# Attention and two feed-forward layers on one core: two totals by accumulating DMA, a second layer without plain products, another plan

## The chip, the cores and the metric

One NeuronCore of a Trainium2 chip. The metric is the device time of one execution in microseconds, as the median of the runs shown.

## What is computed

The inputs are q, k, v of 4 x 8 heads, 576 positions, 64 wide, and a gate value f per position. Attention has a causal mask and a decay from the running sum of log f; its output, 2304 tokens x 512, goes through two feed-forward layers, all in float32:

```
attn  = softmax(scale * q @ k.T + cum[i] - cum[j], causal) @ v
x     = attn.transpose(0, 2, 1, 3).reshape(2304, 512)
h     = x @ w_in            # 512 x 2048
x     = (h - tanh(h)) @ w_out
h     = x @ w_in2
out   = (h * sigmoid(h)) @ w_out2
```

## The kernel before, in words

Every float32 number of a product is split into a high part in TensorE's rounded float32 format and a low rest, and each product is made of three matmuls: high x high, high x low, low x high. ScalarE makes the high part (a cast), VectorE the low one (a subtraction).

**Units.** Each layer (l = 0, 1) is cut into 12 units: four sets s of 512 hidden columns by three blocks b of 768 tokens. Units are numbered 0 to 11 for the first layer and 12 to 23 for the second. A unit has a first product (x by w_in), the gate, and a second product (gate output by w_out), which is added to a total of the block in the big SBUF tile `x`. Both products are done in seven half-size products on 2 x 2 blocks in place of eight, in a scheme of Winograd's kind: sums and differences of the blocks are multiplied, and the products combined. The four quarters of a block are called 11, 12, 21, 22.

**The joint part.** Units 0 to 2 run beside and after the attention in written-out steps. From unit 3 on, `joint()` writes a list of tasks: in the stage that starts at `base[u]`, TensorE does by turns one group of unit u's first product (`h_step`, 12 matmuls of 384 columns) and one group of unit u-1's second product (`c_step`, 12 matmuls of 384 columns in the first layer, 18 of 256 in the second). A stage has 14 such steps. Around them stand the tasks of the other engines: ScalarE copies a bank of partial sums to the other bank (`cp`, `seed`), runs the gate function and casts; VectorE combines gate outputs (`two`), makes low halves, adds to totals (`gain`); both decode the next weights (`decode`, spread over the stage by `spread`).

**The plan.** `planned()` is a list scheduler. It knows a cost per task in steps, what each task reads and writes, and a due time (`latest`) that follows from the step at which TensorE needs the result. It takes tasks in order of time, on each engine the one that is due first among those that are ready; TensorE's and the DMAs' tasks keep their written order. If a task would hold up another that becomes ready during it and is due before its end, the other goes first (`soon`). The result is only an order of instructions on each engine; on the chip, semaphores do the waiting. All DMAs of this part are issued by SP, in the plan's order. The plan starts with every engine free at time 0, though units 0 to 2 still have work in flight there.

**Unit 13 (PLAIN).** Its second product is done with the eight plain half-size products: groups of 24 or 12 matmuls of 256 columns (`plain_c`, line 764), with one weight block of its own (`GROUPS[2][2]`, placed at 11), four gate operands in place of seven, no combinations of gate outputs, and its four totals copied by ScalarE (line 1076). Its stage is one step longer (line 826).

**Between the layers.** The last set of the first layer (units 9 to 11, one per block) ends with four VectorE instructions, `mix` (line 1058): the difference of quarters 22 and 21 into the tile `aside`, 22 plus 12 into 22, and the last partial sums into 12 and 21. SP stores `aside` to DRAM. The stage of unit 12, 13 or 14 then begins with `make` (line 892): it loads `aside` into quarter 11, makes `t` = 12 - 11 and 21 = 21 - t on VectorE (line 900), and splits seven operands into a ring of three tiles (cast at line 915, low half at line 912), each of which SP also stores for later sets (`spill`, line 638). `t` is kept in the tile `f_tmp`, which in the first layer is the temporary of the last two tanh gates of each unit (lines 943, 944). The first second-product group of unit 12 writes the bank that the last two mixes of block 2 read; before it, line 720 sets half of that bank to zero.

Of the kernel before, what the change touches and what calls it, by code (L numbers as in the profile page):

```python
# [7 lines left out]
F32 = mybir.dt.float32  # L8
# [6 lines left out]
P = 128  # L15
B, H, S, D = 4, 8, 576, 64
# [14 lines left out]
NB, TB, TH = 3, 768, 384  # L31
NPR = NFC // 2
NSET = NPR // 2
# [3 lines left out]

U0 = 3
S0 = U0 // 3
PLAIN = (13,)  # L40
PLAINSETS = {s for s in range(NSET, 2 * NSET) if all(NB * s + b in PLAIN for b in range(NB))}
EARLIER = 5
MIXED = {u // NB for u in PLAIN} - PLAINSETS
# [5 lines left out]
def forgetting_attention_two_ffn(  # L49
# [12 lines left out]
    nc = tc.nc  # L62
# [103 lines left out]
    PLUS, MINUS = ALU.add, ALU.subtract  # L166
# [270 lines left out]
    def gather(n):  # L437
        u, h, j, i, g = halves[n]
        l, s, b = units[u]
        acc = accs.pop((u, h, g))  # L440
        t0 = TB * b + TH * h
        if l == 0:
            total, acc = x[:, 2 * g:2 * g + 2, t0:t0 + TH], acc[:, :, 0:TH]
        else:
            total = x[:, 2 * h:2 * h + 2, TB * b + 512 * g:TB * b + 512 * g + (512, 256)[g]]
            total = total.rearrange("p k (t w) -> p k t w", w=256)
            acc = acc[:, 0:2 - g].rearrange("p t (k w) -> p k t w", w=256)
        if s == 0:
            nc.scalar.copy(total, acc)
        else:  # L450
            nc.vector.tensor_tensor(total, acc, total, ALU.add)
# [210 lines left out]
    aside = {}  # L662
# [12 lines left out]
    def aside_load(b, to):  # L675
        nc.sync.dma_start(out=to, in_=aside[b])

    gring = {}

    def gtile(n):  # L680
# [125 lines left out]
    def joint():  # L806
# [6 lines left out]
        def task(when, eng, cost, fn, reads=(), writes=(), keen=False):  # L813

            tasks.append((when, eng, cost, fn, reads, writes, keen))
# [76 lines left out]
        def make(u):  # L892

            b, t0 = units[u][2], base[u]
            at = {"21": (1, 0), "22": (1, 1), "11": (0, 0), "12": (0, 1)}
            q = {c: lambda c=c: xblock(b, *at[c]) for c in at} | {"t": lambda: ftile(u, "tmp")}
            key = dict(zip(q, [("x", b, c) for c in (11, 12, 21, 22)] + ["tmp"]))

            def total(when, to, p, r, op=MINUS):
                task(t0 + when, "V", W2, lambda: tt_(q[to](), q[p](), q[r](), op), (key[p], key[r]), (key[to],))  # L900

            task(t0 - 4, "D", 3, lambda: aside_load(b, q["11"]()), (("t1", b),), (key["11"],))
            total(-1.5, "t", "12", "11")
            total(0, "21", "21", "t")
            src = {1: "11", 2: "21", 6: "t", 3: "12", 7: "22", 5: "11", 4: "21"}
            for k, i in enumerate(STEPS):
                n, f = 7 * (u - U0) + k, src[i]
                kr, when = ("xr", n % 3), t0 + 2 * k - 4.6

                def low(n=n, f=f):  # L910
                    t = ring_tile(n)
                    tt_(t[:, 1], q[f](), rd(t[:, 0]), MINUS)
                    spill(n)

                task(when, "A", N2, lambda n=n, f=f: copy(ring_tile(n)[:, 0], q[f]()), (key[f],), (kr,))
                task(when + 0.1, "V", W2, low, (key[f], kr), (kr,))


        for u in range(U0, len(units) + 1):
            t0 = base[u]  # L920
            if u < len(units):
# [27 lines left out]
                def two(when, to, p, r, op, kt, kp, kr, keen=True):  # L949
                    task(when, "V", W2, lambda: tt_(to, p, r, op), (kp, kr), (kt,), keen)  # L950
# [3 lines left out]
                cp(t0 + 5.05, zs, ys, kz, ky)  # L954
                cp(t0 + 7.05, g12, zs, f12, kz)
                cp(t0 + 9.05, g22, ys, f22, ky)
                two(t0 + 11.05, g22, zs, g22, PLUS, f22, kz, f22)
                two(t0 + 11.5, g12, zs, g12, PLUS, f12, kz, f12)
                gate(t0 + 11.55, g22, g22, f22, f22, True)
                gate(t0 + 12.0, g12, g12, f12, f12, True)  # L960
                if u in PLAIN:
# [78 lines left out]

            if l == 0:
                if s == S0:
                    task(t0 + 3, "V", W2, lambda a=xs[12], c=xs[22]: tt_(a, a, c, MINUS), (kx[12], kx[22]), (kx[12],))
                else:
                    task(t0 + 2, "D", 3, lambda b=b: aside_load(b, aside_tile()), (("t1", b),), ("aside",))
                    task(t0 + 10.9, "A", N2, lambda to=ys: copy(to, aside_tile()), ("aside",), (ky,), True)
                seed(t0 + 2.05)
                gain(t0 + 4.05, 11, zs, kz)
                seed(t0 + 6.05)
                gain(t0 + 8.05, 22, zs, kz)  # L1050
                task(t0 + 8.9, "A", N2, lambda to=zs, frm=xs[12]: copy(to, frm), (kx[12],), (kz,), True)
                gain(t0 + 10.05, 21, ys, ky)
                gain(t0 + 12.05, 12, zs, kz, copies=True)
                if s < NSET - 1:
                    task(t0 + 14.05, "A", N2, lambda frm=ys: copy(aside_tile(), frm), (ky,), ("aside",), True)
                else:
                    def mix(when, to, frm, r, op, keys, kt):
                        task(when, "V", W2, lambda: tt_(to() if callable(to) else to, frm, r, op), keys, (kt,))

                    mix(t0 + 11.5, aside_tile, xs[22], xs[21], MINUS, (kx[22], kx[21]), "aside")  # L1060
                    mix(t0 + 12.5, xs[22], xs[22], xs[12], PLUS, (kx[22], kx[12]), kx[22])
                    mix(t0 + 14.05, xs[12], xs[12], ys, MINUS, (kx[12], ky), kx[12])
                    mix(t0 + 14.06, xs[21], xs[21], ys, PLUS, (kx[21], ky), kx[21])
                task(t0 + (14.5 if s < NSET - 1 else 13), "S", 0, lambda b=b: aside_store(b), ("aside",), (("t1", b),))
                continue
            first = s == 0
            if plain_:
# [59 lines left out]
    def planned(tasks):  # L1127

        LAG, EARLY = 0.1, 8

        def lag(n, d):

            e, f, keen = tasks[n][1], tasks[d][1], tasks[n][6]
            if e == f:
                return 0.06 if e == "V" else 0
            return LAG if keen or e == "P" else LATE.get((f, e), LAG)

        LATE = {("V", "A"): 0.5, ("A", "V"): 0.15, ("P", "A"): 0.1, ("P", "V"): 0.1}
        tasks = sorted(tasks, key=lambda t: t[0])
        writer, readers, deps = {}, {}, []  # L1140
        for n, (when, eng, cost, fn, reads, writes, keen) in enumerate(tasks):
            d = {writer[k] for k in reads if k in writer}
            for k in writes:
                d |= readers.pop(k, set())
                if k in writer:
                    d.add(writer[k])
            d.discard(n)
            deps.append(d)
            for k in reads:
                readers.setdefault(k, set()).add(n)  # L1150
            for k in writes:
                writer[k] = n
        free, end, order = dict.fromkeys("PAVSD", 0.0), {}, []
        queue = {e: [n for n, t in enumerate(tasks) if t[1] == e] for e in free}


        latest = [t[0] if t[1] == "P" else 1e9 for t in tasks]
        for n in reversed(range(len(tasks))):
            for d in deps[n]:
                if tasks[d][1] != "P":  # L1160
                    latest[d] = min(latest[d], latest[n] - lag(n, d) - tasks[d][2])

        def ready(n):
            if all(d in end for d in deps[n]):
                return max([end[d] + lag(n, d) for d in deps[n]] + [tasks[n][0] - EARLY])

        behind = 0
        while any(queue.values()):
            best = None
            for e, waiting in queue.items():  # L1170
                known = [(max(r, free[e]), n) for n in waiting[:1 if e in "PSD" else 60] if (r := ready(n)) is not None]
                if not known:
                    continue
                t = min(known)[0]
                now = [n for r, n in known if r <= t]
                n = min(now, key=lambda n: latest[n])

                soon = [(r, k) for r, k in known if t < r < t + tasks[n][2] - 0.1 and latest[k] + behind < t + tasks[n][2]
                        and latest[n] + behind > r + tasks[k][2]]
                if soon:  # L1180
                    t, n = min(soon)
                if best is None or t < best[0]:
                    best = t, e, n
            t, e, n = best
            if e == "P":
                behind = t - tasks[n][0]
            queue[e].remove(n)
            end[n] = t + tasks[n][2]
            free[e] = t if e == "D" else end[n]
            order.append((t, e != "P", len(order), n))  # L1190
        return [tasks[n][3] for *_, n in sorted(order) if tasks[n][3]]
# [438 lines left out]
```

## Time and profile before

| | us |
|---|---|
| median of 3 runs | 904.29 (904.21 to 904.33) |
| the profiled execution | 904.37 |
| its span, first to last instruction | 902.6 |
| busy: PE | 890.4 (99%) |
| busy: PEld | 845.5 (94%) |
| busy: DVE | 784.9 (87%) |
| busy: ACT | 602.4 (67%) |
| busy: POOL | 161.6 (18%) |

PE is TensorE's matmuls, PEld its weight loads, DVE VectorE, ACT ScalarE, POOL GpSimd, SP the engine that issues DMAs. The profiled execution is one more run; its span leaves out what comes before the first and after the last instruction. The granted clock of TensorE is 1.000 over the whole span. Matmuls are pipelined, and the ends in the rows are modelled, so a matmul's row is longer than the step from one to the next.

### The profile page before, as it was taken

To read this page: it belongs to the slowest core of one execution; us is meant where nothing else is said; L and a number is where in the kernel's file an instruction comes from. 1 tells how busy PE (TensorE), PEld (TensorE's weight loads), DVE (VectorE), ACT (ScalarE), POOL (GpSimd) and SP (SyncE) were. 2 spreads that over 40 slices of the span, in tenths; PEclk is the share of its full clock that TensorE was granted. 3 is DMA by queue.
4 is the path that set the end of the run, shared out by engine and by line. 5 is a ranking of instruction groups with operands and counts; after the bars stand their busy time and mean duration, and the time that the engine had idled before them with its cause. 6 is when DMAs were issued, how large, how long until landed. Compare 5 with 4: busy or idle time off the path is not lost.

```text
span 902.6 us, 16281 instructions
## 1 busy us (share of the span) xinstructions
PE 890.4 (99%) x6080; PEld 845.5 (94%) x6080; DVE 784.9 (87%) x1321; ACT 602.4 (67%) x1006; POOL 161.6 (18%) x242
## 2 busy tenths in 40 slices
PE   8999999999999999999999999999999999999997
PEld 6777777799999999999999999999999999999997
DVE  7799999798889999998999999997897799776647
ACT  6888888765556666766676777866765666555443
POOL 8999999400000000000000000000000000000000
PEclk9999999999999999999999999999999999999999
DMA  5424533567458677787678565677667566555753
GB/s 167 155 98 150 177 119 102 191 250 281 193 224 285 244 264 247 246 296 270 228 275 293 208 243 221 249 252 278 242 239 264 196 234 226 191 191 177 233 169 123
DMA packets 51103, 196.04 MB, mean 217 GB/s; under 512 B 9744, under 2 KB 15120, under 8 KB 50992
## 3 DMA queue, kind: packets, MB, share of 16 engines
q1 hardware_dynamic: 50744, 194.72, 60.9%
q8 instruction: 48, 0.79, 0.3%
q10 hardware_dynamic: 280, 0.28, 0.1%
q14 instruction: 31, 0.25, 0.1%
HBM read 151.98 MB, written 41.88 MB: 215 GB/s over the span
## 4 chain that ended last, share of the span: by engine, by line
PE 94%; DVE 3%; ACT 1%; issue 1%; POOL 0%; DMA 0%; DVEq 0%; POOLq 0%; ACTq 0%
PE h L656 33%; PE a L735 32%; PE t L1362 5%; PE s L1315 5%; PE a L431 5%; PE out_t L1418 5%; PE h L475 3%; PE a L764 2%; PE s L1307 2%; PE h L461 1%; PE out L1418 0%; PE out_t L1446 0%; DVE x L1035 0%; ACT raw L203 0%; DVE gr L991 0%
## 5 line engine op out<-in xcount | busy, mean ns | idle before, releaser
L656 PE MATMUL h<-xr,wh 128*128 128x384 f32 x1176 | 299.0, 335 | 1.0 <-ACT h L947 0.9
L656 PEld LDWEIGHTS h<-xr,wh 128*128 128x128 f32 x1176 | 208.6, 188 | 1.6 <-ACT h L947 1.6
L656 PE MATMUL h<-xr,wl 128*128 128x384 f32 x588 | 196.6, 334 | 0.0
L656 PEld LDWEIGHTS h<-xr,wl 128*128 128x128 f32 x588 | 110.4, 188 | 0.0
L990 ACT CAST gr<-f 128x768 fp32r<-128x768 f32 x104 | 86.8, 838 | 32.5 <-PE a L735 29.8
L991 DVE TENSOR_TENSOR gr<-f,gr 128x768 fp32r<-128x768 f32 x104 | 98.7, 951 | 5.8 <-ACT gr L990 5.7
L735 PE MATMUL a<-wh,gr 128*128 128x256 f32 x516 | 99.2, 282 | 0.0
L735 PEld LDWEIGHTS a<-wh,gr 128*128 128x128 f32 x516 | 82.9, 190 | 0.0
L1336 ACT ACTIVATE p<-p,mn 128x128 f32<-128x128 f32 (+3 forms) x128 | 71.2, 558 | 17.0 <-DVE mn L1328 14.3
L1035 DVE TENSOR_TENSOR x<-a,x 128x768 f32<-128x768 f32 (+1 forms) x64 | 59.3, 929 | 20.7 <-PE a L735 20.5
L735 PE MATMUL a<-weh,gr 128*128 128x256 f32 x384 | 74.0, 282 | 0.3 <-DVE x L1035 0.3
L1350 POOL TENSOR_SCALAR p<-p,sm 128x128 f32<-128x128 f32 (+3 forms) x128 | 73.0, 587 | 7.2 <-DVE sm L1347 6.8
L735 PE MATMUL a<-gr,wh 128*128 128x384 f32 x288 | 73.3, 334 | 0.4 <-DVE gr L991 0.4
L735 PE MATMUL a<-wl,gr 128*128 128x256 f32 x258 | 72.8, 282 | 0.0
L1328 DVE CUSTOM_DVE_ANT_0 p<-s,mask 128x128 f32<-128x128 f32 (+3 forms) x128 | 59.6, 479 | 14.2 <-PE s L1315 14.1
L1027 ACT COPY a<-a 128x768 f32<-128x768 f32 x49 | 38.4, 783 | 47.1 <-PE a L735 45.5
L735 PEld LDWEIGHTS a<-weh,gr 128*128 128x128 f32 x384 | 61.7, 190 | 0.6 <-issue 0.5
L947 ACT COPY h<-h 128x768 f32<-128x768 f32 x42 | 33.0, 786 | 34.7 <-PE h L656 33.5
L735 PE MATMUL a<-gr,weh 128*128 128x384 f32 x216 | 54.8, 334 | 0.0
L735 PE MATMUL a<-wel,gr 128*128 128x256 f32 x192 | 54.2, 282 | 0.0
L1257 POOL TENSOR_TENSOR kqs<-kqraw,kqs 128x288 fp32r<-128x288 f32 (+1 forms) x62 | 53.8, 890 | 1.3
L735 PEld LDWEIGHTS a<-gr,wh 128*128 128x128 f32 x288 | 52.0, 188 | 0.7 <-DVE gr L991 0.7
(169 smaller groups left out, 2070.0 us busy)
## 6 DMA issues: line engine op xcount, KB each, us to landing
xr<-xd SPq DMA_DIRECT2D x126, 768.0 KB
raw<-w_in SPq DMA_DIRECT2D x32, 512.0 KB
raw<-w_out SPq DMA_DIRECT2D x32, 512.0 KB
xd<-xo SPq DMA_DIRECT2D x21, 768.0 KB
xd<-xr SPq DMA_DIRECT2D x21, 768.0 KB
kqraw<-kq SPq DMA_DIRECT2D x16, 608.0 KB
aside<-aside SPq DMA_DIRECT2D x15, 384.0 KB
vraw<-v SPq DMA_DIRECT2D x16, 320.0 KB
```

What stands on the lines that cost most here:

```text
L431: nc.tensor.matmul(dst, w, m, start=first and r == 0, stop=last and r == 2)
L656: nc.tensor.matmul(dst[:, j, 0:TH], w[:, ds], m[:, d], start=i in (1, 5) and d == r == 0, stop=d == 1 and r == 2, skip_group_check=True,)
L735: nc.tensor.matmul(dst, w, m, start=fresh and (l == 0 or d != 1) and j == r == 0, stop=j == 1 and r == 2, skip_group_check=True,)
L990: task(w, "A", N2, lambda g=g, f=frm: copy(g[:, 0], f), (kf,), (("gh", kg),))
L991: task(w + 0.1, "V", W2, lambda g=g, f=frm: tt_(g[:, 1], f, rd(g[:, 0]), MINUS), (kf, ("gh", kg)), (("gl", kg),))
L1035: task(when, "V", n, lambda: tt_(to, *((frm, to) if op == PLUS else (to, frm)), op), (kf, kx[c]), (kx[c],), True)
L1257: eng.tensor_tensor(lo[:, c0:c1], raw[p][:, c0:c1], rd(hi[:, c0:c1]), ALU.subtract)
L1315: nc.tensor.matmul(s[:, h, c:c + n], a[half(h), q], b[half(h), 0:n], start=r == 0, stop=r == 3,)
L1328: nc.vector.tensor_tensor_reduce(out=pt.rearrange("p (g c) -> p g c", g=2) if i == 4 else pt, in0=src, in1=m, op0=ALU.add, op1=ALU.min, sc ...
L1336: nc.scalar.activation(pt, pt, AF.Exp, bias=mn, scale=-1.0, accum_out=sums[:, n // 3 % 5, n % 3, 0:1],)
L1350: nc.gpsimd.tensor_scalar(pt, pt, sm[:, j:j + 1], 1.0, ALU.mult, ALU.mult)
L1362: nc.tensor.transpose(t[:, k], pt[:, c * P:c * P + P], ident)
```

## The change

Unit 13 becomes a unit like its neighbours: seven products, three combinations, no weight block of its own, a stage of 14 steps.

Between the layers, quarter 22 is now kept with the opposite sign through the first layer, so that the sums needed are sums: `side(b, 1)` in DRAM is quarter 22 stored, and quarter 21 added to it by an accumulating DMA from GpSimd; `side(b, 2)` is the new quarter 22 (12 - 22) stored, and `side(b, 1)` added to it, from DRAM to DRAM. `make` loads the first into quarter 11 and the second as `t`. Two VectorE instructions per block go, `aside` and the making of `t`. Signs are turned where quarter 22 is read, among them one operation of the second layer's combinations.

The planner has a queue "G" for GpSimd's DMAs, starts VectorE at 2.0 and ScalarE at 0.8 steps, and its `soon` rule now adds up the tasks that become ready during a task, in order of due time: if one of them would be late, the earliest ready of those late goes first, unless the task itself is due before all of these are done.

```diff
-PLAIN = (13,)
+PLAIN = ()
...
-        if s == 0:
+        if (l, s, g, h) == (0, 0, 0, 1):
+            nc.scalar.mul(total, acc, -1.0)
+        elif s == 0:
...
+    def side(b, i):
+        if (b, i) not in sides:
+            sides[b, i] = dram.tile([P, 2, TH], F32, name=f"side{b}_{i}")
+        return sides[b, i]
...
-            task(t0 - 4, "D", 3, lambda: aside_load(b, q["11"]()), (("t1", b),), (key["11"],))
-            total(-1.5, "t", "12", "11")
+            def load(when, i, c):
+                task(t0 + when, "D", 3, lambda: nc.sync.dma_start(out=q[c](), in_=side(b, i)), (("side", b, i),), (key[c],))
+
+            load(-4, 1, "11")
+            load(-1.5, 2, "t")
             total(0, "21", "21", "t")
...
-                two(t0 + 11.05, g22, zs, g22, PLUS, f22, kz, f22)
-                two(t0 + 11.5, g12, zs, g12, PLUS, f12, kz, f12)
+                two(t0 + 11.05, g22, g22, zs, (PLUS, MINUS)[l], f22, kz, f22)
+                two(t0 + 11.5, g12, g12, zs, (PLUS, MINUS)[l], f12, kz, f12)
...
-                    task(t0 + 3, "V", W2, lambda a=xs[12], c=xs[22]: tt_(a, a, c, MINUS), (kx[12], kx[22]), (kx[12],))
+                    task(t0 + 3, "V", W2, lambda a=xs[12], c=xs[22]: tt_(a, a, c, PLUS), (kx[12], kx[22]), (kx[12],))
...
-                gain(t0 + 8.05, 22, zs, kz)
+                gain(t0 + 8.05, 22, zs, kz, MINUS)
...
-                    mix(t0 + 11.5, aside_tile, xs[22], xs[21], MINUS, (kx[22], kx[21]), "aside")
-                    mix(t0 + 12.5, xs[22], xs[22], xs[12], PLUS, (kx[22], kx[12]), kx[22])
+                    def put(when, i, key, frm, op=None):
+                        eng, queue, cost = ("G", nc.gpsimd, 2.5) if op else ("D", nc.sync, 2)
+                        more = {"accum_op": op, "max_dma_last_dim": 4 * TH} if op else {}
+                        task(when, eng, cost, lambda b=b: queue.dma_start(out=side(b, i), in_=frm() if callable(frm) else frm, **more),
+                             (key,), (("side", b, i),))
+
+                    put(t0 + 8.5, 1, kx[22], xs[22])
+                    put(t0 + 10.5, 1, kx[21], xs[21], PLUS)
+                    mix(t0 + 12.5, xs[22], xs[12], xs[22], MINUS, (kx[22], kx[12]), kx[22])
+                    put(t0 + 13.5, 2, kx[22], xs[22])
+                    put(t0 + 15, 2, ("side", b, 1), lambda b=b: side(b, 1), PLUS)
                     mix(t0 + 14.05, xs[12], xs[12], ys, MINUS, (kx[12], ky), kx[12])
                     mix(t0 + 14.06, xs[21], xs[21], ys, PLUS, (kx[21], ky), kx[21])
-                task(t0 + (14.5 if s < NSET - 1 else 13), "S", 0, lambda b=b: aside_store(b), ("aside",), (("t1", b),))
+                if s < NSET - 1:
+                    task(t0 + 14.5, "S", 0, lambda b=b: aside_store(b), ("aside",), (("t1", b),))
...
-        free, end, order = dict.fromkeys("PAVSD", 0.0), {}, []
+        free, end, order = dict.fromkeys("PAVSDG", 0.0) | {"V": 2.0, "A": 0.8}, {}, []
...
-                soon = [(r, k) for r, k in known if t < r < t + tasks[n][2] - 0.1 and latest[k] + behind < t + tasks[n][2]
-                        and latest[n] + behind > r + tasks[k][2]]
-                if soon:
-                    t, n = min(soon)
+                soon = sorted((latest[k], k, r) for r, k in known if t < r < t + tasks[n][2] - 0.1)
+                then, hurt = t + tasks[n][2], []
+                for due, k, r in soon:
+                    if due + behind < then:
+                        hurt.append((r, k))
+                    then += tasks[k][2]
+                if hurt and latest[n] + behind > min(hurt)[0] + sum(tasks[k][2] for r, k in hurt):
+                    t, n = min(hurt)
```

## Rows read from the trace of the kernel before

**Rows 1.** The page, busy us, share of the span and instructions

```profile
PE 890.4 (99%) x6080; PEld 845.5 (94%) x6080; DVE 784.9 (87%) x1321; ACT 602.4 (67%) x1006; POOL 161.6 (18%) x242
```

**Rows 2.** Waits of PEld from 230 us on: total us, times, longest

```profile
PEld h L656 <- ACT h L947: 1.6, 2, 1.3
PEld a L720 <- DVE x L1058: 1.5, 1, 1.5
PEld a L735 <- DVE gr L991: 0.7, 1, 0.7
```

**Rows 3.** Windows: us, then busy us (instructions) by engine, clock, DMA share, GB/s

```profile
553.00:584.00 31.00, 29.81 (x212) 29.49 (x212) 30.66 (x39) 23.47 (x32) 0.00 (x0) 1.00 0.61 239
584.00:615.00 31.00, 31.00 (x224) 31.00 (x224) 29.63 (x41) 22.89 (x31) 0.00 (x0) 1.00 0.75 261
615.00:645.00 30.00, 30.00 (x215) 30.00 (x215) 21.93 (x28) 19.44 (x24) 0.00 (x0) 1.00 0.74 258
```

**Rows 4.** Chain of waits in order of time: start us, us, what

```profile
585.89 2.87 PE a L764 x24
...
590.84 1.43 PE a L764 x12
...
611.29 4.31 PE a L764 x36
...
617.68 2.15 PE a L735 x18
```

**Rows 5.** Groups by line and shape: count | busy us, mean ns | idle before

```profile
L991 DVE TENSOR_TENSOR gr<-f,gr 128x768 fp32r<-128x768 f32 x104 | 98.7, 951 | 5.8 <-ACT gr L990 5.7
...
L990 ACT CAST gr<-f 128x768 fp32r<-128x768 f32 x104 | 86.8, 838 | 32.5 <-PE a L735 29.8 <-DVE f L944 1.6 <-PE h L735 0.6
...
L207 DVE TENSOR_SCALAR wa<-raw 128x1024 uint32<-128x1024 uint32 x29 | 19.9, 687 | 3.4 <-ACT raw L203 3.3
...
L950 DVE TENSOR_TENSOR f_a<-f,f 128x768 f32<-128x768 f32 x20 | 19.0, 952 | 0.2
...
L249 DVE TENSOR_TENSOR wl<-ws,wh 128x256 fp32r<-128x256 f32 x14 | 5.9, 419 | 0.0
```

**Rows 6.** Timeline of VectorE at the end of unit 11: start us, us, instruction

```profile
540.53 0.95 DVE L1035 TENSOR_TENSOR x<-a,x 128x768 f32<-128x768 f32 x1
...
545.13 0.95 DVE L1035 TENSOR_TENSOR x<-a,x 128x768 f32<-128x768 f32 x1
...
551.87 0.95 DVE L1058 TENSOR_TENSOR x<-x 128x768 f32<-128x768 f32 x1
...
553.88 1.81 DVE L1058 TENSOR_TENSOR x<-x,a 128x768 f32<-128x768 f32 x2
```

**Rows 7.** Timeline of PEld there, with the idle time before

```profile
555.74 0.30 PEld L720 LDWEIGHTS a<-wh,gr 128*128 128x128 f32 x2 [1.51 <-DVE x L1058]
```

**Rows 8.** Waits of the SP queue, whole span: total us, times, longest

```profile
SPq L676 <- DMA aside<-aside: 33.5, 6, 6.6
...
SPq L1622 <- DMA out<-x: 2.0, 1, 2.0
```

**Rows 9.** Timelines of DVE, ACT and PEld around the making of unit 12's `t`

```profile
523.39 0.95 DVE L944 TENSOR_TENSOR f<-f,f_tmp 128x768 f32<-128x768 f32 x1
...
527.54 0.84 ACT L915 CAST xr<-f_tmp 128x768 fp32r<-128x768 f32 x1
...
529.58 0.95 DVE L912 TENSOR_TENSOR xr<-f_tmp,xr 128x768 fp32r<-128x768 f32 x1
...
530.63 0.36 PEld L656 LDWEIGHTS h<-xr,wh 128*128 128x128 f32 x2
```

**Rows 10.** Timeline of ScalarE, at 269 and at 530 us

```profile
269.10 2.19 ACT L203 ACTIVATE raw<-raw 128x1024 f32<-128x1024 f32 x2
...
271.90 0.80 ACT L947 COPY h<-h 128x768 f32<-128x768 f32 x1
...
529.78 1.28 ACT L940 ACT_TABLE_LOAD   x1
```

More of the change, by code (lines that the diff above doesn't have):

```diff
@@ L676, in aside_load @@
         nc.sync.dma_start(out=to, in_=aside[b])
+    sides = {}
+    def side(b, i):
+        if (b, i) not in sides:
+            sides[b, i] = dram.tile([P, 2, TH], F32, name=f"side{b}_{i}")
+        return sides[b, i]
     gring = {}
@@ L1057, in mix @@
                     def mix(when, to, frm, r, op, keys, kt):
-                        task(when, "V", W2, lambda: tt_(to() if callable(to) else to, frm, r, op), keys, (kt,))
-                    mix(t0 + 11.5, aside_tile, xs[22], xs[21], MINUS, (kx[22], kx[21]), "aside")
-                    mix(t0 + 12.5, xs[22], xs[22], xs[12], PLUS, (kx[22], kx[12]), kx[22])
+                        task(when, "V", W2, lambda: tt_(to, frm, r, op), keys, (kt,))
+                    def put(when, i, key, frm, op=None):
[8 more added lines that the diff above has]
+                    put(t0 + 15, 2, ("side", b, 1), lambda b=b: side(b, 1), PLUS)
                     mix(t0 + 14.05, xs[12], xs[12], ys, MINUS, (kx[12], ky), kx[12])
                     mix(t0 + 14.06, xs[21], xs[21], ys, PLUS, (kx[21], ky), kx[21])
-                task(t0 + (14.5 if s < NSET - 1 else 13), "S", 0, lambda b=b: aside_store(b), ("aside",), (("t1", b),))
+                if s < NSET - 1:
+                    task(t0 + 14.5, "S", 0, lambda b=b: aside_store(b), ("aside",), (("t1", b),))
                 continue
@@ L1170, in planned @@
             for e, waiting in queue.items():
-                known = [(max(r, free[e]), n) for n in waiting[:1 if e in "PSD" else 60] if (r := ready(n)) is not None]
+                known = [(max(r, free[e]), n) for n in waiting[:1 if e in "PSDG" else 60] if (r := ready(n)) is not None]
                 if not known:
```

## The prediction

> **What bounds the kernel now.** I read the page's busy shares first, then the waits of TensorE, then the chain of waits step by step, and last the timelines around each wait. TensorE is busy for 99% of the span [rows 1], at one steady pace. In the joint part (from 258 us on) its weight-load side waits in only three places that matter: 1.6 us for ScalarE's copy of a bank (L947), 1.5 us for VectorE's last mix between the layers (L1058), 0.7 us for a VectorE low half (L991) [rows 2]. That is 3.8 us in 640. So the end is set by how many matmuls there are, plus those few waits; an instruction on another engine counts only where it makes a new wait. The next engine is VectorE: from 553 to 615 us, the stretch of unit 13, it is busy 30.66 and 29.63 of 31 us, so 0.34 + 1.37 = 1.7 us are free there; the 30 us after it have 8.1 us free [rows 3].
>
> **Matmuls (unit 13, no plain second product).** The chain shows the plain stage as three groups of 24 matmuls at 2.87 us, three of 12 at 1.43 us and one of 36 at 4.31 us; a normal unit has seven groups of 18 at 2.15 us [rows 4]. Old: 3 x 2.87 + 3 x 1.43 + 4.31 = 17.21 us. New: 7 x 2.15 = 15.05 us. The seven groups of the first product between them stay. Gain 2.16 us, on the path, since TensorE runs without a gap through this stage.
>
> **What unit 13 gets instead.** VectorE gains 8 instructions: three combinations of gate outputs and one subtraction from the last (each L950's kind), three more low halves (seven operands for four) and one subtraction into a total. At 0.95 us [rows 5] that is 7.6 us. In the same stretch go two totals of `make` (units 13 and 14, L900, 2 x 0.95 us) and two low halves of the extra weight block (2 x 0.42 us): 2.7 us. Net +4.9 us against 1.7 us free: 3.2 us too much, unless the decoding of the next weights moves behind 615 us, where 8.1 us are free. The planner picks by due time, so most of it should move. Bounds: 0 (all moves; it cannot be a gain, since work is only added) and 3.2 us; I take 1.2 us of new waits, a bit over a third. ScalarE gets three casts, three seeds and four totals for four copies: six more, at a cast's 0.84 us each 5 us, in a stretch where it is busy 22.89 of 31 us [rows 3, 5]; its 8 us of idle time hide them, and only if VectorE's delays use those up is it late.
>
> **Between the layers (units 9 to 11, `make` of 12 to 14).** Per block two VectorE subtractions of 0.95 us go (`aside` and `t`), 5.7 us in all from 490 to 585 us. Added per block: two stores and one load on SP, two accumulating transfers on POOL, which does nothing else after the attention (x0 in every stretch of [rows 3]); POOL's waits delay nobody but its own second transfer. The SP store in the old place goes too.
>
> The waits that this adds sit on VectorE. The mix into x22 must wait until store 1 has read x22; the mix into x21 until the accumulating transfer has read x21. Behind each are queued the low half for TensorE's next first product (L912) and all else on VectorE. For block 2 there is no slack: TensorE's first second-product group of unit 12 (L720) already waits for the x21 mix. Its times: x22 is final at 541.48, x21 at 546.08, the mixes run from 553.88 to 555.69 [rows 6], and the weights of L720 load at 555.74 after 1.51 us of waiting, so they could at 554.23 [rows 7]. A 384 KB store has a row: SP sat from the issue of an `aside` store until it had landed, 33.5 us over six times, 5.6 us each, at most 6.6; the shortest landing in these rows is 2.0 us, a store at the very end [rows 8]. So store 1 lands at 541.5 + 5.6 = 547.1; the x22 mix (before: 551.87) is covered by almost 5 us. The accumulating transfer starts then, lands L later, and the x21 mix ends about 1.0 us after that. L up to 554.2 - 547.1 - 1.0 = 6.1 us costs nothing, L = 7.6 us keeps today's wait. No row shows L. From below 2.0 us; from above I take two of the longest landings, 13.2 us, because such a transfer must also read what it adds to and is issued by an engine whose issue the trace does not show. Nearest row: 5.6 us. I take 6.6 us, half a microsecond of wait, so 1.0 of the 1.5 us goes: gain 1.0, bounds gain 1.5 and loss 5.6 us (L = 13.2: 561.3 - 554.2 = 7.1, less 1.5).
>
> In the Trainium skill, "DMA: Bandwidth & Descriptors", section "Anatomy of one DMA — SWDGE (gpsimd) path", gives about 2.0 us plus size over 436 GB/s for a transfer issued by GpSimd: an estimate of 2.9 us for 384 KB, with which the whole 1.5 us would go and the sum below be 0.5 us lower; the store's 5.6 us, on another queue and in traffic, speaks for more. Against the change speaks the Trainium skill's "SBUF — State Buffer", section "SBUF: two separate sides": GpSimd cannot write descriptors while VectorE runs an instruction in a two-port mode. The trace's candidates are short, the weight shifts at 0.69 us for 1024 elements against 0.95 us for 768 of a two-input one [rows 5], so each would delay L by at most 0.69 us: an estimated 0.7 us on the sum.
>
> **The load of `t` (unit 12 only).** The tile is also the temporary of the tanh gates, free at 523.39 + 0.95 = 524.34. Today `t` goes through the cast (from 527.54) and the low half (from 529.58) to a first-product group whose weights load at 530.63 [rows 9]. Loaded, it needs 524.34 + landing + 0.84 + 0.95: on time up to 4.5 us of landing, 2.1 us late at 6.6. I take 0, since VectorE is an instruction earlier here; bounds 0 and 2.1 us. For units 13 and 14 the tile is free early. What the SP queue holds behind this load is `make`'s spills, whose ring tiles have two groups (4 us) of cover.
>
> **The plan.** New starting times for VectorE and ScalarE, and a rule that sums the work that a long task would delay. It can remove the worse of the first two waits: at 269.10 ScalarE ran two weight scalings (2.19 us) ahead of the bank copy that came at 271.90 [rows 10], 1.3 of the 1.6 us [rows 2]. I take 1.3 gained, bounds 1.6 gained and 1.5 lost (another such inversion elsewhere, the longest wait in the rows). The 0.7 us before L735 follow a table load of 1.28 us on ScalarE that the plan does not know [rows 10], and VectorE's relief touches only its last link: gain 0.3 of 0.7, no loss taken beyond that of the plan.
>
> At nothing: changed signs (same instruction, other operation; three copies become scalings on ScalarE in the early part), the subtraction into a basis that unit 16 no longer needs (0.95 us off VectorE, hidden).
>
> **Sum.** 904.37 (this execution) - 2.16 + 1.2 - 1.0 - 1.3 - 0.3 = 900.8 us. The median shown is 904.29, 0.08 lower: 900.7 us predicted.
>
> **Rivals.**
> 1. The plan does not do what it says: the waits move but stay as long in total (3.8 us). For it: every order on VectorE and ScalarE changes, and both bounds of the plan's term are near. Against: two of the three waits have a cause that the change addresses. 904.29 - 2.16 = 902.1 us (901.3 to 903.3).
> 2. VectorE becomes the bound in unit 13: the 3.2 us are not deferred and stand as waits, the old waits stay, or half of them: 904.29 - 2.16 + 3.2 = 905.3, or 903.4. For it: 97% busy there. Against: 8.1 us free right behind.
> 3. Slower: the accumulating transfer of block 2 holds the x21 mix. With the other waits unchanged, more than 2.16 + 1.8 us must come on top of today's 1.5, so L above 7.6 + 4.0 = 11.6 us decides it. At L = 13.2: 904.29 - 2.16 + 5.6 = 907.7 us; blocks 0 and 1 have two groups (4.2 us) more slack and would add up to 2.9 us each, 913.5. For it: two landings in series and an operation that the trace never shows. Against: twice the longest landing is needed.
>
> **Chances.** Forecast (899.3 to 902.0) 0.48; rival 1 0.22; rival 2 0.16; rival 3 0.11; the rest 0.03. This kernel's measurements can tell about 0.2% (1.8 us) from no change: faster is below 902.5, slower above 906.1. Faster: 0.48 + 0.16 of rival 1 + 0.02 = 0.66; same: 0.06 + 0.15 + 0.01 = 0.22; slower 0.12. The range goes from all old waits gone and no new one, 904.29 - 2.16 - 3.8 = 898.3, to rival 2's 905.3, taken as 905.4.
>
> **What would show it.** Right: no line L764; seven groups of 18 at 2.15 us in unit 13; the wait of L656 for L947 near 265 to 273 us shorter; L720's wait under 1 us. Wrong: VectorE waiting at L1058's place for a DMA, with L720 behind it (rival 3); TensorE waiting for low halves L991 or combinations between 580 and 615 us (rival 2); waits of 3.8 us or more in new places (rival 1). A wait of L656 for a low half just after 530 us would say that `t` lands late.

## The result, and the profile after

The changed kernel takes 910.36 us (909.91 to 912.13, four runs) against 904.31 us: 6.05 us more, a ratio of 1.0069 with a 95% interval of 1.0057 to 1.0082. Forecast were 900.7 us and a range up to 905.4 us.

The profiled execution of the changed kernel is the slowest of the four, 912.13 us, with a span of 910.4 us, 7.8 us above the span before. First the page's busy row:

```profile
PE 892.0 (98%) x6062; PEld 845.9 (93%) x6062; DVE 785.3 (86%) x1320; ACT 605.5 (67%) x1010; POOL 167.6 (18%) x248
```

18 matmuls fewer than in [rows 1], as worked out. The waits of the weight loads, which answer to [rows 2] (waits of the attention part left out; total us, times, longest):

```profile
PEld a L745 <- ACT a L1041: 6.9, 2, 4.7
...
PEld a L745 <- DVE gr L1005: 2.2, 2, 1.9
...
PEld h L658 <- DVE xr L925: 1.2, 1, 1.2
...
PEld h L658 <- ACT h L960: 0.4, 1, 0.4
...
PEld h L658 <- ACT f L960: 0.2, 1, 0.2
...
PEld h L658 <- DVE wl L249: 0.2, 1, 0.2
```

That is 11.1 us for 3.8 before. (L1041 is the seed copy, L1027 before; L745 was L735, L1005 L991, L925 L912, L960 L947, L1073 L1058.) The chain of waits shows who stands behind them:

```profile
482.29 7.58 DMA side<-x
...
490.48 10.51 DMA side<-x
...
501.01 0.95 DVE x L1073
...
504.96 3.89 PE a L745 x11
508.85 2.86 PE h L658 x12
...
524.18 9.34 DMA side<-x
...
539.80 6.86 DMA xd<-xr
...
547.42 0.80 ACT a L1041
548.22 0.04 issue
548.27 2.35 PE a L745 x12
```

Read from the top: in block 0 the store of quarter 22 lands after 7.58 us, the accumulating transfer behind it after 10.51 us, then comes the x21 mix, the seed, the operands, TensorE. In block 1 the transfer takes 9.34 us, and VectorE waits 2.08 us for it. From there VectorE works without a gap up to the low half of `t`, for which TensorE waits 1.2 us (L925 above); ScalarE's cast of `t` had ended before, at 538.30 us (timelines of VectorE and ScalarE):

```profile
533.61 1.82 DVE L1073 TENSOR_TENSOR x<-x,a 128x768 f32<-128x768 f32 x2 [2.08 <-DMA side<-x]
...
537.46 0.84 ACT L928 CAST xr<-f_tmp 128x768 fp32r<-128x768 f32 x1 [1.15 <-DMA f_tmp<-side]
...
538.82 0.95 DVE L925 TENSOR_TENSOR xr<-f_tmp,xr 128x768 fp32r<-128x768 f32 x1
```

The spill of that low half (`xd<-xr`) lands after 6.86 us; ScalarE's next cast waits for it, with the seed queued behind, and so TensorE waits again, 2.1 us at 548 us. VectorE's timeline in block 0 has the other half (idle time and its end in brackets):

```profile
480.02 0.94 DVE L1049 TENSOR_TENSOR x<-x,a 128x768 f32<-128x768 f32 x1
...
484.02 0.95 DVE L1049 TENSOR_TENSOR x<-a,x 128x768 f32<-128x768 f32 x1
...
501.01 0.95 DVE L1073 TENSOR_TENSOR x<-x,a 128x768 f32<-128x768 f32 x1 [6.37 <-DMA side<-x]
```

Quarters 22 and 21 are final at 480.96 and 484.97; the mix that must wait until quarter 21 has been read runs at 501.01. Two groups of matmuls are slow afterwards (in the chain above), 3.89 us for 11 and 2.86 us for 12 where 12 take 2.08 us. TensorE had stood still from 498 to 505 us but for one matmul, and its clock fell to the lower level, 1.2 GHz, for a while: columns 1, 2 and 3 are stretch, length and TensorE's busy time, then the granted clock, the DMA engines' busy share and GB/s:

```profile
490.00:500.00 10.00, 8.49 (x49) 1.00 1.05 312
500.00:505.00 5.00, 0.48 (x2) 0.86 0.93 272
505.00:512.00 7.00, 7.00 (x26) 0.61 0.13 23
512.00:520.00 8.00, 8.00 (x48) 1.00 0.59 197
```

The sum closes: -2.16 (matmuls) + 11.1 - 3.8 (waits) + 2.8 (lower clock: 3.89 + 2.86 - 1.91 - 2.08) = +7.9 us, for 7.8 us of span.

The wait for which I had worked out the price is not there. L720 of [rows 7] (L730 now) does not wait at all: block 2's transfer, issued at 556.22, landed within 4.9 us:

```profile
DMA to landing us min/median/max: 4.9/4.9/4.9
```

What differs is the traffic. The stretches of store and transfer in block 0 (first two rows), of the transfer in block 1 and of store and transfer in block 2, all engines, granted clock, DMA share and GB/s last:

```profile
482.00:490.00 8.00, 8.00 (x48) 8.00 (x47) 7.43 (x10) 4.47 (x7) 0.00 (x0) 1.00 0.89 305
490.50:501.00 10.50, 7.99 (x47) 7.67 (x45) 4.15 (x5) 2.20 (x3) 1.27 (x1) 1.00 1.05 317
...
524.00:533.50 9.50, 9.50 (x57) 9.50 (x56) 7.20 (x8) 7.08 (x11) 1.10 (x1) 1.00 1.01 316
551.60:556.00 4.40, 4.40 (x27) 4.40 (x26) 4.37 (x7) 3.97 (x6) 0.00 (x0) 1.00 0.68 267
556.20:561.00 4.80, 4.80 (x29) 4.80 (x28) 4.80 (x7) 4.21 (x6) 1.10 (x1) 1.00 0.74 153
```

In blocks 0 and 1 the DMA engines are full (0.89 to 1.05); in block 2, 0.68 to 0.74, since units 12 to 14 make their operands and load none (`ring_load` skips them).

### The profile page after: what moved, and what is told of

It reads as the page before. It is cut to its first block, busy times and chain, and to the rows that moved or that the text cites. A ratio compares the mean times of both kernels' runs of the same rounds, so it can differ in the third digit from the quotient of the medians.

```text
span 910.4 us, 16283 instructions
## 1 busy us (share of the span) xinstructions
PE 892.0 (98%) x6062; PEld 845.9 (93%) x6062; DVE 785.3 (86%) x1320; ACT 605.5 (67%) x1010; POOL 167.6 (18%) x248
## 4 chain that ended last, share of the span: by engine, by line
PE 91%; DMA 4%; DVE 3%; issue 1%; POOL 0%; ACT 0%; DVEq 0%; SPq 0%; POOLq 0%; ACTq 0%
PE a L745 32%; PE h L658 32%; PE a L431 5%; PE t L1391 5%; PE s L1344 5%; PE out_t L1447 5%; PE h L477 3%; DMA side<-x 3%; PE s L1336 2%; PE h L463 2%; DMA xd<-xr 1%; DVE gr L1005 0%; DVE x L1049 0%; PE out L1447 0%; PE out_t L1475 0%
## 5 line engine op out<-in xcount | busy, mean ns | idle before, releaser
L745 PE MATMUL a<-wh,gr 128*128 128x256 f32 x564 | 108.5, 282 | 0.0
L1005 DVE TENSOR_TENSOR gr<-f,gr 128x768 fp32r<-128x768 f32 x105 | 99.5, 951 | 4.2 <-ACT gr L1004 4.2
L745 PEld LDWEIGHTS a<-wh,gr 128*128 128x128 f32 x564 | 90.6, 190 | 0.0
L745 PE MATMUL a<-gr,wh 128*128 128x384 f32 x288 | 75.2, 340 | 7.8 <-ACT a L1041 6.2
L745 PE MATMUL a<-weh,gr 128*128 128x256 f32 x420 | 81.1, 283 | 0.3 <-DVE x L1049 0.3
L745 PE MATMUL a<-wl,gr 128*128 128x256 f32 x282 | 79.6, 282 | 0.0
L1041 ACT COPY a<-a 128x768 f32<-128x768 f32 x52 | 40.8, 784 | 49.2 <-PE a L745 39.7
L1049 DVE TENSOR_TENSOR x<-a,x 128x768 f32<-128x768 f32 (+1 forms) x55 | 50.7, 924 | 21.2 <-PE a L745 21.1
L1078 POOL DMA_DIRECT2D side<-x x3 | 3.5, 1167 | 355.6 <-DMA side<-x 317.5
L745 PEld LDWEIGHTS a<-weh,gr 128*128 128x128 f32 x420 | 67.5, 190 | 0.7 <-issue 0.5
L745 PEld LDWEIGHTS a<-gr,wh 128*128 128x128 f32 x288 | 52.9, 191 | 9.1 <-ACT a L1041 6.9
L960 ACT COPY h<-h 128x768 f32<-128x768 f32 x42 | 33.0, 786 | 42.4 <-PE h L658 41.2
L745 PE MATMUL a<-wel,gr 128*128 128x256 f32 x210 | 59.2, 282 | 0.0
L745 PE MATMUL a<-gr,weh 128*128 128x384 f32 x216 | 54.9, 334 | 0.0
```

Of the source, the lines that this page charges most:

```text
L745: nc.tensor.matmul(dst, w, m, start=fresh and (l == 0 or d != 1) and j == r == 0, stop=j == 1 and r == 2, skip_group_check=True,)
L1005: task(w + 0.1, "V", W2, lambda g=g, f=frm: tt_(g[:, 1], f, rd(g[:, 0]), MINUS), (kf, ("gh", kg)), (("gl", kg),))
L1049: task(when, "V", n, lambda: tt_(to, *((frm, to) if op == PLUS else (to, frm)), op), (kf, kx[c]), (kx[c],), True)
```

## The experiments

The theory after the result: the accumulating transfers land late and hold VectorE, and ScalarE behind it. The rivals: the new plan, or VectorE's load in unit 13. Times below are medians, and each ratio is to the kernel before, run on the same chip.

**Each part alone.** First the change without accumulating transfers (`no_accum`):

```diff
-                    put(t0 + 8.5, 1, kx[22], xs[22])
-                    put(t0 + 10.5, 1, kx[21], xs[21], PLUS)
+                    mix(t0 + 11.5, aside_tile, xs[22], xs[21], PLUS, (kx[22], kx[21]), "aside")
...
-                    put(t0 + 13.5, 2, kx[22], xs[22])
-                    put(t0 + 15, 2, ("side", b, 1), lambda b=b: side(b, 1), PLUS)
+                    task(t0 + 13, "S", 0, lambda b=b: nc.sync.dma_start(out=side(b, 1), in_=aside_tile()), ("aside",), (("side", b, 1),))
...
-            load(-1.5, 2, "t")
+            total(-1.5, "t", "12", "11", PLUS)
```

> The change with its two totals per block made by VectorE again (one sum into the aside tile, stored by SP and loaded into quarter 11; t from it on VectorE); seven products in unit 13, turned signs and the new plan stay. Theory (the accumulating transfers land late and hold VectorE's x21 mix and the making of t): 899 to 901 us, TensorE's three long waits between 490 and 550 us gone, no stretch at the lower clock. Rival (the new plan or the fuller unit 13 is to blame): 905 us or more.

903.72 us, ratio 0.9992 (0.9983 to 1.0001): between the two. 6.6 us of the result come from the transfers, but the gain behind them is 0.6 us, not 4. The waits:

```profile
PEld h L658 <- ACT f L960: 1.8, 1, 1.8
PEld a L730 <- DVE x L1073: 1.4, 1, 1.4
PEld h L658 <- DMA xr<-xd: 1.0, 1, 1.0
PEld h L658 <- DVE xr L925: 0.6, 1, 0.6
```

The waits for L960, for the operand load and for L925 stand between 609 and 624 us, at unit 13's end. `only_accum` is the mirror image: the changed kernel with `PLAIN = (13,)`, the old start and the old rule of the plan.

> The kernel before with the accumulating transfers and turned signs alone: unit 13 plain, the old start and the old rule of the plan. Theory: slower than before by the transfers' price, 908 to 914 us, with VectorE waiting for the accumulating transfer of quarter 21 in blocks 0 and 1 for 2 to 7 us. Rival (plan or unit 13): 903 to 905.5 us.

909.80 us, 1.0065 (1.0052 to 1.0077), as the theory has it; VectorE waits 6.4 us for the transfer of quarter 21 in two places. `only_seven` has `PLAIN = ()` in the kernel before:

> The kernel before with seven products in unit 13 and nothing else. Theory (matmuls set the pace, VectorE can put its decoding off): 904.3 - 2.16 = 902.1 us, 901 to 903.5. Rival (VectorE is the bound in unit 13): 904.5 to 906 us with TensorE waiting between 580 and 615 us.

904.67 us, 1.0004 (0.9995 to 1.0013): the rival is right. Two new waits stand at 608 and 611 us, and VectorE is full in that stretch (waits, then the window, and the one from 615 us on):

```profile
PEld a L735 <- DVE gr L991: 1.8, 1, 1.8
...
PEld h L656 <- ACT f L947: 0.9, 1, 0.9
```

```profile
584.00:612.00 28.00, 25.68 (x180) 25.27 (x179) 27.63 (x38) 21.82 (x29) 0.00 (x0) 1.00 0.56 207
...
615.00:645.00 30.00, 30.00 (x215) 29.86 (x214) 25.92 (x34) 22.19 (x30) 0.00 (x0) 1.00 0.82 296
```

2.7 us of new waits cancel 2.16 us of matmuls; the 0.7 us wait of [rows 2] is gone from this profile, so its span, 902.4 us, is 0.2 us below the one before. `only_plan` has the new start and the new `soon` rule alone:

> The kernel before with the plan's starting times and its new rule alone. Theory: the first two waits (1.6 us) mostly go, the others stay: 902.5 to 903.5 us. Rival (the plan moves waits or adds some): 904 us or more.

903.08 us, 0.9986 (0.9977 to 0.9995), as expected; of the 1.6 us of L656 for L947, 0.4 us are left, the others stay. The three parts alone come to +5.5, +0.4 and -1.2 us, 4.7 together; the change costs 6.05, and no run says where the remaining 1.4 us come from.

**Is it VectorE's load in unit 13?** `left_out_t` is `no_accum` without the two instructions that make `t` for units 13 and 14:

```diff
-            total(-1.5, "t", "12", "11", PLUS)
+            if not b:
+                total(-1.5, "t", "12", "11", PLUS)
```

> The run without accumulating transfers (903.7 us) with the two VectorE instructions that make t for units 13 and 14 left out (their t is old data); no DMA is added. Theory (VectorE's load in unit 13 eats the gain of the seven products, and two instructions are enough to give most of it back): the 3.8 us of waits between 608 and 624 us fall below 1.5 us, 900.5 to 902 us. Rival (the waits are a matter of the plan's order): 903 us or more.

900.74 us, 0.9960 (0.9946 to 0.9974): two VectorE instructions of 0.95 us are worth 3.0 us here. Between 607 and 624 us TensorE now waits 0.6 us. It is load, and two instructions are enough to decide it; `t_accum_12` below takes the same two from VectorE in another way and comes to the same time. `seven_pool` meant to show the same with the work kept, on GpSimd:

```diff
-                    tt_(t[:, 1], q[f](), rd(t[:, 0]), MINUS)
+                    (nc.gpsimd.tensor_tensor if b == 2 else tt_)(t[:, 1], q[f](), rd(t[:, 0]), MINUS)
...
-                task(when + 0.1, "V", W2, low, (key[f], kr), (kr,))
+                task(when + 0.1, "G" if b == 2 else "V", 1 if b == 2 else W2, low, (key[f], kr), (kr,))
```

> The run without accumulating transfers (903.7 us), with the seven low halves that make unit 14's operands moved from VectorE to GpSimd, which is idle there: 6.7 us less on VectorE before 612 us. Theory (VectorE has no room in unit 13; its decoding is due by unit 15 and can not be put off): the waits of 3.8 us between 608 and 624 us mostly go, 900 to 901.5 us. Rival (those waits are an unlucky order of the plan, not load): they stay or come back elsewhere, 903 to 904.5 us.

907.57 us, 1.0035 (1.0021 to 1.0048): neither. The waits at 608 to 624 us went, but GpSimd's timeline shows that one of its subtractions took 9.72 us instead of 1.85, and TensorE waited 5.1 us for it, until 595.3 us. Then TensorE ran at the lower clock until 600 us (1.2 GHz, a granted clock of 0.50 in the window below). So it decides nothing on load.

```profile
577.36 1.85 POOL L925 TENSOR_TENSOR xr<-x,xr 128x768 fp32r<-128x768 f32 x1 [3.10 <-ACT xr L928]
585.54 9.72 POOL L925 TENSOR_TENSOR xr<-f_tmp,xr 128x768 fp32r<-128x768 f32 x1 [6.33 <-ACT xr L928]
```

```profile
595.30:600.00 4.70, 4.69 (x16) 4.69 (x17) 1.04 (x1) 0.71 (x2) 4.49 (x2) 0.50 0.68 272
```

**What makes the transfer late?** `plain_pool` sends quarter 21 from GpSimd to another DRAM tile, without adding (quarter 21 is left out of the first total):

```diff
-                    put(t0 + 10.5, 1, kx[21], xs[21], PLUS)
+                    task(t0 + 10.5, "G", 2.5, lambda b=b: nc.gpsimd.dma_start(out=side(b, 3), in_=quarter(NB * (NSET - 1) + b, 21)), (kx[21],), (("side", b, 1),))
```

> The change with the accumulating transfer of quarter 21 replaced by a plain transfer of the same bytes, issued by GpSimd at the same place to another DRAM tile (so quarter 21 is left out of the first total). Theory a (the adding makes it slow): it lands in 4 to 6 us in blocks 0 and 1 too, and the time falls below 905 us. Theory b (the other transfers in flight make it slow): it lands in 8 to 10 us like the accumulating one, and the time stays at 907 us or more.

899.98 us, 0.9951 (0.9933 to 0.9969). But it told a (the adding makes it slow) and b (the traffic does) apart badly: the transfer takes 7.4 and 7.5 us to land in blocks 0 and 1 and 3.0 us in block 2, yet it also no longer waits for the store and starts at 485.28 instead of 490.48. So I ran `overwrite`, which keeps the place, the wait and the order and drops only the adding (quarter 22 is left out of the first total):

```diff
-                        more = {"accum_op": op, "max_dma_last_dim": 4 * TH} if op else {}
+                        more = {"accum_op": op, "max_dma_last_dim": 4 * TH} if op and i == 2 else {}
```

> The change with the same instructions in the same order, but the transfer of quarter 21 from GpSimd a plain one that overwrites the stored quarter 22 instead of adding to it (so quarter 22 is left out of the first total); it still waits for the store. Theory (most of the lateness is two landings in series in full DMA queues): it still lands in 6 to 9 us in blocks 0 and 1, about 2 us sooner than the adding one, and the time is 904 to 908 us. Rival (it is the adding): it lands in 3 to 5 us and the time falls to 900 to 902 us.

903.88 us (900.66 to 905.92), 0.9991 (0.9978 to 1.0004): just below what the theory gave, and above the rival. The ten runs differ by more than 5 us; the two fastest have a granted clock of 1.000, the profiled one (905.15 us) 0.997. In its chain the transfer of block 0 takes 7.97 us, where the adding one took 10.51, TensorE still waits 1.7 and 1.9 us, and the group behind runs slowly (chain, then waits):

```profile
490.07 7.97 DMA side<-x
...
498.06 0.95 DVE x L1073
...
502.01 3.45 PE a L745 x11
```

```profile
PEld a L745 <- DVE gr L1005: 2.3, 2, 1.9
...
PEld a L745 <- ACT a L1041: 1.7, 1, 1.7
```

In block 1 it lands in 7.5 us, the adding one in 9.3; in block 2 in 3.4, the adding one in 4.9. So both rows of the chain matter. The second landing in full queues is 8 us without any adding, past what this place can hide. The adding comes on top, 1.5 to 2.5 us per transfer: without it TensorE's waits fall from 11.1 to 4.8 us, by 3.0 us in block 0, and the two waits of 1.2 and 2.1 us behind block 1 are gone. That is 6.3 of the 7.0 us between the two profiled spans; the medians differ by 6.5. How the adding and the traffic share the lateness is less sure: the adding transfer of block 0 landed in 7.9 us in `copy_aside` and in 10.8 us in `copy_t2` below. VectorE's work, the prediction's other candidate, can't be what delayed it in the changed kernel: VectorE was idle for 6.4 of those 10.5 us.

**A version in which VectorE waits for no transfer.** `copy_aside`: ScalarE copies quarter 21 into the free tile `aside`, and the transfer reads that. `t` of unit 12 is VectorE's again, and the second total's store and transfer are left out for block 0.

```diff
-                    put(t0 + 10.5, 1, kx[21], xs[21], PLUS)
+                    task(t0 + 11, "A", N2, lambda f=xs[21]: copy(aside_tile(), f), (kx[21],), ("aside",), True)
+                    put(t0 + 11.5, 1, "aside", aside_tile, PLUS)
...
-            load(-1.5, 2, "t")
+            if b:
+                load(-1.5, 2, "t")
+            else:
+                total(-1.5, "t", "12", "11", PLUS)
```

> The change with quarter 21 first copied by ScalarE into the aside tile, and the accumulating transfer reading that copy, so that no VectorE instruction waits for it; t of unit 12 made by VectorE, of units 13 and 14 by accumulating transfers. Theory (it is the wait of the x21 mix, not the transfer itself, that costs): no wait of TensorE over 2 us at 500 us, no lower clock, 900 to 903.5 us. Rival (the accumulating transfers slow the other DMAs and so the kernel): 906 us or more with TensorE or ScalarE waiting for DMAs.

900.25 us, 0.9960 (0.9947 to 0.9972): faster than before by 4.0 us, with the adding transfers still slow (7.9 and 9.4 us to land in blocks 0 and 1). It is the wait that cost, not the transfer. The profiled execution is the slowest of the five, 902.02 us; in it one wait of 2.8 us is left, behind a spill, in ScalarE's timeline:

```profile
537.11 0.83 ACT L931 CAST xr<-x 128x768 fp32r<-128x768 f32 x1 [4.24 <-DMA xd<-xr]
537.85 0.79 ACT L1044 COPY a<-a 128x768 f32<-128x768 f32 x1
```

`t_accum_12` lets VectorE make the first total and uses accumulating transfers for `t` of units 13 and 14 only (the edits of `no_accum` for the first total, of `copy_aside` for `t`).

> The change with the first total made and stored as before (VectorE, aside tile), and only t of units 13 and 14 made by accumulating transfers, whose source is in DRAM. Theory: nothing on VectorE waits for them; 902 to 904 us, near the run without accumulating transfers, less the two VectorE instructions that go. Rival (accumulating transfers cost by their traffic): over 905 us.

900.93 us, 0.9966 (0.9953 to 0.9978), better than expected, and within 0.2 us of `left_out_t`, where the two instructions are left out and no transfer replaces them. Two variants of `copy_aside` try its last wait: the second total's transfer 5 steps later (`put(t0 + 20, ...)`), and that transfer for unit 14 alone (`if b == 2`).

> The copy_aside run (900.25 us) with the accumulating transfer of the second total planned 5 steps (10 us) later, out of the way of unit 12's spills. Theory (its 3 us wait at 538 us comes from a spill that lands late beside that transfer): that wait shrinks to 1 us or less, 898 to 900 us. Rival (the spills are late for another reason): 900 to 901 us.

> The copy_aside run with t by an accumulating transfer for unit 14 alone, by VectorE for units 12 and 13: one transfer and one store less at 528 us, one VectorE instruction more. Theory: the wait at 538 us shrinks, those at 608 us come back a little, 899 to 901 us. Rival: 900.2 us or above with the wait at 538 us unchanged.

900.31 us (0.9957, 0.9944 to 0.9970) and 900.26 us (0.9956, 0.9942 to 0.9970). In both profiles the wait shrank, to 1.1 and 0.3 us, but the medians stayed. `copy_late` tests nothing: GpSimd has only these transfers, so a later step in the plan leaves their order, and in the traces every engine runs the same instructions in the same order in `copy_aside` and `copy_late`. The transfer in question is issued at 528.14 us in the one and at 528.79 us in the other (GpSimd's timelines):

```profile
528.14 0.96 POOL L1081 DMA_DIRECT2D side<-side  x1 [9.21 <-DMA side<-x]
```

```profile
528.79 0.96 POOL L1081 DMA_DIRECT2D side<-side  x1 [9.89 <-DMA side<-x]
```

So 2.8 and 1.1 us are two executions of one program, 902.02 and 900.31 us long, and what makes that spill late is not shown. `copy_t2` does drop the transfer and store at 528 us, but its 0.3 us is one execution as well. Of the waits at 608 us, 0.3 us came back (at 606 and 612 us). The medians do not tell the three versions apart. The waits left in `copy_t2`:

```profile
PEld a L745 <- ACT a L1044: 0.8, 3, 0.3
PEld a L730 <- DVE x L1076: 0.5, 1, 0.5
PEld a L745 <- issue: 0.5, 1, 0.5
PEld h L658 <- ACT h L963: 0.4, 1, 0.4
```

## Why the prediction was wrong

**The step that failed** is the term of the accumulating transfer: "I take 6.6 us ... gain 1.0". Its size was off, and with it the place. L, the time from issue to landing, was 10.5 and 9.3 us in blocks 0 and 1. Store 1, put at 5.6 us from [rows 8], took 7.6 us. Those rows are SP's waits, which begin only when the issue is over; from issue to landing one of these stores took 7.2 us already (380.49 to 387.74 us in the trace before). In block 0 store 1 also left SP 1.3 us late (482.29 for 480.96), behind two operand loads that waited on SP for TensorE:

```profile
477.71 4.48 SPq L627 DMA_DIRECT2D xr<-xd  x2
```

From quarter 22 final to quarter 21 read I had 12.2 us; block 0 needed 20.0 (480.96 to 500.99). TensorE's group there was ready at 498.2 us, and the landing came 1.9 us before the weight load that waited for it (500.99 to 502.89), so there was room until 496.3; for the low half behind it (L1005, 1.9 us more of waiting), which comes 4.0 us after the landing on a VectorE without a gap, until 494.4. I had seen that blocks 0 and 1 have two groups more slack, and took block 2 as the place that decides. But the times I had taken were block 2's, where the queues were emptiest. There L was 4.9 us, and the 1.5 us wait went. In place of the gain of 1.0 us, TensorE waited 6.6 us in block 0 and 3.3 us behind block 1.

This is rival 3 in mechanism and in time (907.7 to 913.5 us), at a chance of 0.11; its decision point, L above 11.6 us in block 2, was not what decided it, and of its sign, VectorE waiting for a DMA with L720 behind, the first half came, with other groups behind. The term's bounds went to L = 13.2 us, a loss of 5.6 us, but the stated range ended at rival 2's 905.4 us and left this case out; the chance was too small.

The plan had the same error: it counts 2 steps for the store and 2.5 for the transfer, about 9.4 us at 2.08 us a step, for what took 18.1 us. No run gives it the measured landings, so how much another order on VectorE would hide is open.

**Not in the sum:** the lower clock after the waits, 2.8 us in the profiled execution.

**The matmuls** came as worked out (2.16 us; seven groups of 2.15 us).

**Unit 13:** rival 2 is true by itself. I took 1.2 us of 3.2 us for new waits; `only_seven` has 2.7 us there, which eat the whole gain. Work did move behind 615 us: VectorE is busy 25.92 us there in `only_seven`, 21.93 in [rows 3]. The waits stand all the same, at 608 and 611 us: room behind a stretch does not help what is due inside it. In the changed kernel these waits are 0.3 us, with two VectorE instructions of `make` less before them. The earlier standstill, in which VectorE could catch up, is not needed for that: `left_out_t` and `plain_pool` have none, and 0.6 and 0.35 us of such waits.

**The load of `t`** was taken as 0, with a bound of 2.1 us. Issued at 530.29, it landed about 7.1 us later, and TensorE waited 1.2 us for L925 at 539.83. But what ended last before that low half was VectorE's work behind the late transfer, not the load: without the load's lateness the wait would be the same, without the transfer's some 0.7 us (an estimate: the cast ended at 538.30). In `overwrite` and `only_accum` the load takes 6.0 and 6.3 us and TensorE does not wait for it. The spill behind it, which I had called covered by two groups, landed after 6.86 us and cost another 2.1 us at 548 us.

**The plan's** term was right: 1.3 us forecast for the first waits, 1.2 us measured for the plan alone. The wait before L735 stayed in `only_plan` (0.8 us), where I had taken 0.3 off.

## What to carry to other kernels

A transfer that reads a buffer puts a wait on the next writer of that buffer; its price is the landing in the traffic of that stretch, so take landings from the busiest of the places where it will run, and count two in series as two. If an in-order engine on the path must wait for it, let an engine with idle time copy the source first: 0.8 us on ScalarE per block, with one total back on VectorE, turned a loss of 6 us into a gain of 4. And count on nothing to be hidden in a stretch where the second engine is 97% busy: here the work removed from the first engine came back as waits for the second. Last, before a variant is credited with what its profile shows, see that the order of instructions changed, and compare the profiled execution with the median.

## What the runs showed of the hardware that was not expected

A plain 384 KB transfer from GpSimd took 3.0 and 3.4 us to land at a DMA share of 0.56 and 0.60 (block 2 of `plain_pool` and `overwrite`) and 7.4 to 8.0 us at 0.97 to 1.01 (their blocks 0 and 1). One that adds to DRAM took 4.9 and 5.1 us in block 2 (shares 0.74 and 0.76, changed kernel and `only_accum`); in blocks 0 and 1 (shares 0.84 to 1.05) it took anything from 5.1 us (`only_accum`, block 1) to 10.8 us (`copy_t2`, block 0):

```profile
DMA to landing us min/median/max: 10.8/10.8/10.8
```

What sets it within that range is open. The Trainium skill's formula in "DMA: Bandwidth & Descriptors", section "Anatomy of one DMA — SWDGE (gpsimd) path", comes to an estimate of 2.9 us: it agrees with the first two and with none in full queues.

A subtraction of 128 x 768 on GpSimd, 1.85 us elsewhere, took 9.72 us at 585.54 us, while VectorE was running without a break, two-input instructions but for one of 0.68 us. The Trainium skill's "SBUF — State Buffer", section "SBUF: two separate sides", says that a GpSimd instruction that reads SBUF and a VectorE instruction with two SBUF inputs lock each other out; the row is of that kind, but the six others in the same run took 1.9 to 2.4 us, so what sets it off is open.
